# A decode layer whose queries come from a register-addressed loop on TensorE, with two score chunks of the last head rebalanced towards TensorE

**Chip, cores, metric.** One NeuronCore of one Trainium2 chip. Times are device microseconds (us) of one execution; "span" is the time from the first to the last instruction of an execution, 1.7 to 3.0 us shorter. All timed runs told here were in the fast state, at a mean granted TensorE clock of 0.87 to 0.89; e8 and e10 are single runs, whose state can't be told, at 0.88.

## The reference

One decode step: layer norm, attention of one query row over a cache of 32 heads, 32,768 positions and 192 channels, output projection, and a two-layer MLP. All data is bf16.

```python
B, Sq, D = 1, 1, 640;  H, Sk, Dh = 32, 32768, 192;  Dff = 1536
q = (layernorm(x) @ wq).reshape(H, Dh)                  # 640 x 6144 weights
scores = einsum("hd,hkd->hk", q, k_cache) * Dh**-0.5
o = einsum("hk,hkd->hd", softmax(scores), v_cache)
h = x + o.reshape(1, H * Dh) @ wo
out = h + relu(layernorm(h) @ w1) @ w2
```

Keys and values are read once, about 805 of the 825 MB that the kernel loads.

## The kernel before

Everything arrives through one queue of loads, issued in program order by SyncE; a load that overwrites a tile waits for that tile's last reader, and all loads behind it wait too (head 0's second keys are issued at 32.97 us, after the query matmuls, and the load behind them at 33.34). Each head's scores are computed in chunks, and in each chunk some columns are multiplied and reduced on the vector engine while the others are transposed and multiplied on TensorE (with copies by ScalarE).

The query weights borrow tiles that keys and values need shortly after:

```python
wq_c = [kt[1][:, c * H * Dh:(c + 1) * H * Dh] for c in range(DT - 1)] + [va[:, 0:H * Dh]]   # DT = 5 rows
```

so head 0's second half of the keys, which goes to `kt[1]`, waits for `att0`, a signal that comes after the last query matmul:

```python
def keys(h, ld):
    if h > 0:
        ...
        g.wait("scs", h - 1, 4 * ld + 3)
    elif ld == 1:
        g.wait("att0")
    load(kt[ld][:], rows(k_hd, h, P * JK * ld, JK), f"dk{ld}", "k", h, ld)

# order of issue
for c in range(DT):
    load(wq_c[c], ...)                    # five rows of query weights
for h in range(LAST):
    keys(h, 0); vals(h, 0); keys(h, 1)    # head 0's keys(0, 1) is the one that waits
    ...
```

The queries are 5 x 64 matmuls of one column each, unrolled; each loads 96 columns of weights:

```python
for c in range(DT):
    g.wait("wq", c)
    calls = [mmul(o_ps[0:HE, 2*h+e:2*h+e+1], wq_c[c][:, h*Dh+e:(h+1)*Dh:2], xn[:, c:c+1], ...)
             for h in range(H) for e in range(2)]
```

The last head has chunks of its own (tile, offset, columns, columns on TensorE); the even ones up to chunk 3 have 16 on TensorE and 16 on the vector engine:

```python
ends = [(c // 2, (c % 2) * J, J, JPS[c % 2] if c > 3 else 16) for c in range(NC - 2)]   # J = 32, JPS = (20, 16)
ends += [(NL - 1, 0, 20, 12), (NL - 1, 20, 20, 12), (NL, 0, 16, 8), (NL + 1, 0, 8, 8)]
```

TensorE's program there ends with the value matmuls of chunks 5, 6 and 7, then the last softmax denominator (`den`), then chunks 8 and 9.

Of the kernel before, what the change touches and what calls it, by code (L numbers as in the profile page):

```python
# [80 lines left out]
def kernel(  # L81
# [16 lines left out]
    _, H, Sk, Dh = A_k_cache.shape  # L98
# [6 lines left out]
    DT = D // P  # L105
# [3 lines left out]
    J = 32  # L109
    JPS = (20, 16)  # L110
    HE = Dh // 2
    NK = Sk // (P * JK)
    NL = Sk // (P * JL)
    NC = 2 * NL
# [6 lines left out]
    full = [(c // 4, (c % 4) * J, J, JPS[c % 2]) + ((c // 2, (c % 2) * J) if c < 4 else (2, (c - 4) * J)) for c in range(NC)]  # L121

    ENDJ = (40, 16, 8)
    ends = [(c // 2, (c % 2) * J, J, JPS[c % 2] if c > 3 else 16) for c in range(NC - 2)]
    ends += [(NL - 1, 0, 20, 12), (NL - 1, 20, 20, 12), (NL, 0, 16, 8), (NL + 1, 0, 8, 8)]
    ends = [q + q[0:2] for q in ends]
    assert sum(ENDJ) == JL
# [23 lines left out]
    def sbuf(name, shape, dtype, align=32):  # L151
        return ctx.enter_context(nc.sbuf_tensor(name, shape, dtype, align_bytes=align))

    def psum(name, shape, dtype=f32):
        return ctx.enter_context(nc.psum_tensor(name, shape, dtype))


    kt = [sbuf(f"kt{i}", [P, JK * Dh], bf16, 512) for i in range(NK)]
    va = sbuf("va", [P, JK * Dh], bf16, 512)
# [12 lines left out]
    wide = sbuf("wide", [P, HE + P + 2 * (P - HE)], bf16)  # L172
# [16 lines left out]
    ln_t = {}  # L189
    for tag in ("ln1", "ln2"):  # L190
# [3 lines left out]
                         xn=sbuf(f"xn_{tag}", [P, DT], bf16))  # L194
    tp = [psum(f"tp{i}", [P, 4, P]) for i in range(TP)]
    sp = psum("sp", [P, 512])
    o_ps = psum("o_ps", [P, 512])
# [4 lines left out]
    wq_c = [kt[1][:, c * H * Dh:(c + 1) * H * Dh] for c in range(DT - 1)] + [va[:, 0:H * Dh]]  # L202
# [21 lines left out]
    sems = {n: nc.alloc_semaphore(n) for n in names}  # L224
# [90 lines left out]
    def pool_program(g):  # L315
        e = nc.gpsimd
        g.do(lambda: e.memset(wide[:], 0.0), "pool_act", ("ident0",))
        g.wait("ident0")
        g.do(lambda: e.affine_select(out=wide[:], in_=wide[:], compare_op=A.not_equal, fill=1.0, base=HE,
                                     pattern=[[-1, HE + P + 2 * (P - HE)]], channel_multiplier=1), "pool_row", ("ident",))  # L320
        def key(h, ld):
            relay(g, "k", h, ld)
            g.do(lambda: nc.gpsimd.sem_inc(sems["pool_dve"], 1))  # L323
            book_relay(g, "k", h, ld, sem="pool_dve")

        for h in range(LAST):
            key(h, 0)
            relay(g, "v", h, 0)
            key(h, 1)
            for ld in ((2, 1) if h == 0 else (1, 2)):  # L330
                relay(g, "v", h, ld)
            relay(g, "W", h)
        key(LAST, 0)
        relay(g, "v", LAST, 0)
        key(LAST, 1)
        key(LAST, 2)
        relay(g, "v", LAST, 1)

    def relay(g, *label):
        if label[0] != "W":  # L340
            g.wait(*label)
        elif label[1] % 2 == 0:
            g.wait("wo", label[1] // 2)
        g.do(lambda: nc.gpsimd.sem_inc(sems["pool_pe"], 1))  # L344
        book_relay(g, *label)

    def book_relay(g, *label, sem="pool_pe"):
        if g.planning:
            n = g.book["count"].get(sem, 0) + 1
            g.book["count"][sem] = n  # L350
            g.book["at"][("at" if sem == "pool_pe" else "atd",) + label] = (sem, n)
# [4 lines left out]
    def pe_group(g, calls, label, sem="pe"):  # L356
        for fn in calls[:-1]:
            g.do(fn)
        g.do(calls[-1], sem, label)

    def mmul(o, w, r, **kw):
        return lambda: pe.matmul(o, lhsT=w, rhs=r, **kw)  # L362
# [105 lines left out]

    def queries(g):

        for c in range(DT):
            g.wait("wq", c)
            calls = [mmul(o_ps[0:HE, 2 * h + e:2 * h + e + 1], wq_c[c][:, h * Dh + e:(h + 1) * Dh:2],
                          ln_t["ln1"]["xn"][:, c:c + 1], start=(c == 0 and h == 0 and e == 0),
                          stop=(c == DT - 1 and h == H - 1 and e == 1), skip_group_check=True)
                     for h in range(H) for e in range(2)]
            if c < DT - 1:
                for fn in calls:
                    g.do(fn)
            else:  # L480
                pe_group(g, calls, ("q",), "pe_act")

    def q_spread(g, h, turn=None):

# [42 lines left out]
    def pe_start(g):  # L527
        g.wait("identf")
        g.wait("x")
        cols = [x_row[0:1, c:D:DT] for c in range(DT)] + [x_row[0:1, c * P:(c + 1) * P] for c in range(DT)]  # L530
        pe_group(g, [mmul(mm[:, i:i + 1], col, ident_b[0:1, 0:1], start=True, stop=True) for i, col in enumerate(cols)],
                 ("xT",), "pe_dve")
        pe_norm(g)
        g.wait("xn", "ln1")
        queries(g)
        pe_group(g, [mmul(attT[:, 0:DT], ident_b, zero5[:], start=True, stop=False, skip_group_check=True)],
                 ("att0",))
        g.wait("qe")
        q_spread(g, 0)
# [255 lines left out]
    for f in (dma_program, pool_program):  # L795
        f(plan)
# [14 lines left out]
    at = book["at"]  # L811
    ends_at, step = {}, {}
    for e in parts:
        far = {s: 0 for s in TAKEN[e]}
        ends_at[e] = []
        for h in range(LAST):
            for label in logs[e][h]:
                s, n = at[label]
# [11 lines left out]
    def looped(e, eng):  # L830
        start, head, end = parts[e]
        g = Program(book, sems, eng)

        def take(amounts):
            g.flush()
            for s, n in amounts.items():
                eng.sem_inc(sems[s], -n)
                g.sub[s] = g.seen[s] = g.sub.get(s, 0) + n

        start(g)  # L840
        head(g, 0)
        take(ends_at[e][0])
        with eng.Fori(0, LAST - 1) as i:
            if e == "pe":
                head(g, 1, i + 2)
            else:
                head(g, 1)
            take(step[e])
        for s in TAKEN[e]:
            g.sub[s] = g.seen[s] = ends_at[e][LAST - 1][s]  # L850
        g.links = dict(links[e])
        end(g)
        g.flush()

    with nc.Block(name="decode_blk", no_gpsimd_drain=True) as block:
        @block.sync
        def _(eng):
            dma_program(Program(book, sems, nc.sync))

        @block.gpsimd  # L860
        def _(eng):
            pool_program(Program(book, sems, nc.gpsimd))

        @block.scalar
        def _(eng):
            looped("act", nc.scalar)

        @block.vector
        def _(eng):
            looped("dve", nc.vector)  # L870

        @block.tensor
        def _(eng):
            looped("pe", nc.tensor)
# [34 lines left out]
```

## Time and profile before

| | before |
|---|---|
| time, median of the 3 runs at hand for the prediction | 1918.84 us (1917.25 to 1919.17) |
| span of the profiled execution | 1915.5 us |
| loaded | 824.97 MB, one queue, 431 GB/s over the span |
| query matmuls | 7.17 to 32.9 us |
| second half of head 0's keys issued | 32.97 us |

How to read it: the queue of loads is full from the first slice to the last (its packets fill 99.8% of the sixteen engines' span), so the time is the bytes, plus any moment in which nothing is queued, plus the tail after the last landing. Two places matter to the change: the moment at which SyncE may issue the second keys, compared with the moment at which the earlier loads run out, and the tail. The lines that show both stand in the prediction.

### The profile page before, as it was taken

To read this page: it belongs to the slowest core of one execution; us is meant where nothing else is said; L and a number is where in the kernel's file an instruction comes from. 1 tells how busy PE (TensorE), PEld (TensorE's weight loads), DVE (VectorE), ACT (ScalarE), POOL (GpSimd) and SP (SyncE) were. 2 spreads that over 40 slices of the span, in tenths; PEclk is the share of its full clock that TensorE was granted. 3 is DMA by queue.
4 is the path that set the end of the run, shared out by engine and by line. 5 is a ranking of instruction groups with operands and counts; after the bars stand their busy time and mean duration, and the time that the engine had idled before them with its cause. 6 is when DMAs were issued, how large, how long until landed. Compare 5 with 4: busy or idle time off the path is not lost.

```text
span 1915.5 us, 36089 instructions
## 1 busy us (share of the span) xinstructions
PE 1554.6 (81%) x15890; PEld 1091.6 (57%) x15890; DVE 1563.2 (82%) x732; ACT 938.5 (49%) x1998; POOL 1.0 (0%) x6
## 2 busy tenths in 40 slices
PE   7878888887888778887878787878788787777888
PEld 7555555555665555655556555545565555555565
DVE  2797787987878978789787888878798787987897
ACT  2455454554544544545545445445355454554444
POOL 0000000000000000000000000000000000000000
PEclk9888888888978889888899888899888898888988
DMA  9999999999999999999999999999999999999998
GB/s 409 430 434 432 430 438 429 437 435 433 432 434 431 435 432 429 437 430 438 434 430 434 434 432 437 431 429 437 429 437 436 430 436 431 434 433 432 431 432 366
DMA packets 29633, 825.27 MB, mean 431 GB/s; under 512 B 3115, under 2 KB 4652, under 8 KB 8108
## 3 DMA queue, kind: packets, MB, share of 16 engines
q1 hardware_dynamic: 29610, 824.98, 99.8%
q8 instruction: 14, 0.23, 0.0%
q14 instruction: 7, 0.06, 0.0%
q10 hardware_dynamic: 2, 0.00, 0.0%
HBM read 824.97 MB, written 0.00 MB: 431 GB/s over the span
## 4 chain that ended last, share of the span: by engine, by line
DVE 42%; DMA 37%; PE 14%; ACT 5%; issue 1%; DVEq 0%; POOLq 0%; SPq 0%
DMA kt<-in_A_k_cache_dram 35%; DVE sc L701 20%; DVE pr L698 20%; PE tp L381 7%; PE o_ps L362 6%; ACT kT L605 4%; DMA va<-in_A_v_cache_dram 2%; DVE o_pair L713 1%; PE sp L362 1%; ACT pA L620 0%; DVE oT L723 0%; DMA kt<-in_A_wq_dram 0%; DVE rec L706 0%; DVE rec L707 0%; DVE odd L719 0%
## 5 line engine op out<-in xcount | busy, mean ns | idle before, releaser
L698 DVE TENSOR_TENSOR pr<-kt,qb 128x3072 f32<-128x3072 bf16 (+2 forms) x257 | 757.5, 2947 | 314.9 <-POOLq L323 286.8
L605 ACT COPY kT<-tp 128x1024 bf16<-128x1024 bf16 (+1 forms) x897 | 813.8, 1018 | 272.1 <-PE tp L381 272.1
L381 PE MATMUL tp<-ident_f,kt 128*128 128x128 f32 x3453 | 592.3, 333 | 237.8 <-POOLq L344 162.9
L701 DVE TENSOR_REDUCE sc<-pr 128x16 f32<-128x3072 f32 (+2 forms) x257 | 756.8, 2945 | 8.9
L381 PEld LDWEIGHTS tp<-ident_f,kt 128*128 128x128 f32 x3453 | 489.0, 172 | 287.0 <-POOLq L344 168.9
L362 PE MATMUL o_ps<-va,pB 128*2 128x384 bf16 x1150 | 218.4, 337 | 62.4 <-POOLq L344 62.4
L362 PEld LDWEIGHTS sp<-qm,kT 128*128 128x128 bf16 x6906 | 197.6, 98 | 83.4 <-issue 43.7
L362 PE MATMUL sp<-qm,kT 128*128 128x2 bf16 x6906 | 214.6, 164 | 25.6 <-ACT pB L611 24.3
L362 PE MATMUL o_ps<-vb,pB 128*2 128x384 bf16 x1152 | 214.4, 332 | 22.5 <-ACT pA L620 21.9
L620 ACT ACTIVATE pA<-sc 128x16 bf16<-128x16 f32 (+2 forms) x257 | 58.2, 227 | 350.0 <-DVEq L65 350.0
L611 ACT ACTIVATE pB<-sp 128x16 bf16<-128x16 f32 (+2 forms) x258 | 52.4, 203 | 309.7 <-PE sp L362 309.7
L362 PEld LDWEIGHTS o_ps<-va,pB 128*2 128x2 bf16 x1150 | 93.3, 85 | 156.4 <-POOLq L344 70.0
L362 PE MATMUL o_ps<-va,pA 128*2 128x384 bf16 x898 | 173.5, 335 | 0.0
L362 PE MATMUL o_ps<-vb,pA 128*2 128x384 bf16 x896 | 167.9, 328 | 0.0
L362 PEld LDWEIGHTS o_ps<-vb,pB 128*2 128x2 bf16 x1152 | 90.1, 84 | 122.3 <-ACT pA L620 27.5
L362 PEld LDWEIGHTS o_ps<-va,pA 128*2 128x2 bf16 x898 | 77.6, 86 | 76.6 <-issue 10.2
L362 PEld LDWEIGHTS o_ps<-vb,pA 128*2 128x2 bf16 x896 | 75.6, 84 | 71.2 <-issue 1.5
L611 ACT ACTIVATION_READ_ACCUMULATOR pB<-sp 128x1 f32 x258 | 55.1, 214 | 0.0
L620 ACT ACTIVATION_READ_ACCUMULATOR pA<-sc 128x1 f32 x257 | 53.1, 206 | 0.0
L362 PE MATMUL o_ps<-xn_ln,kt 128*96 128x1 bf16 (+1 forms) x316 | 22.4, 208 | 2.6 <-DMA kt<-in_A_wq_dram 2.6
L362 PEld LDWEIGHTS o_ps<-xn_ln,kt 128*96 128x96 bf16 (+1 forms) x316 | 22.2, 176 | 2.8 <-issue 2.7
L713 DVE TENSOR_SCALAR o_pair<-o_ps,rec 2x384 bf16<-2x384 f32 x32 | 19.4, 605 | 2.7 <-PE o_ps L362 1.7
(69 smaller groups left out, 186.7 us busy)
## 6 DMA issues: line engine op xcount, KB each, us to landing
kt<-in_A_k_cache_dram SPq DMA_DIRECT2D x62, 6144.0 KB, 26.7
vb<-in_A_v_cache_dram SPq DMA_DIRECT2D x63, 3072.0 KB, 19.3
va<-in_A_v_cache_dram SPq DMA_DIRECT2D x31, 6144.0 KB, 26.8
kt<-in_A_k_cache_dram SPq DMA_DIRECT2D x3, 3072.0 KB, 22.8
wo_s<-in_A_wo_dram SPq DMA_DIRECT2D x16, 480.0 KB, 19.0
kt<-in_A_wq_dram SPq DMA_DIRECT2D x4, 1536.0 KB, 10.8
va<-in_A_v_cache_dram SPq DMA_DIRECT2D x1, 3072.0 KB, 32.1
va<-in_A_v_cache_dram SPq DMA_DIRECT2D x2, 1536.0 KB, 37.0
```

Of the source, the lines that this page charges most:

```text
L362: return lambda: pe.matmul(o, lhsT=w, rhs=r, **kw)
L381: calls.append(lambda b=b, o=o: pe.transpose(out=dst[:, b, :], in_=src[:, o:o + 2 * P].bitcast(f32), identity=ident_f[:]))
L605: g.do(lambda: act.copy(out=kT[c % 2][:, b0:b0 + nb, :], in_=src[:, 0:nb, :].bitcast(bf16)), "act_pe", ("cp", h, c, k))
L611: g.do(lambda: act.activation(out=pB[c % NB][:, 0:jp], in_=sp[:, 0:jp], func=F.Exp, scale=SCALE, accum_out=dsums[:, 2 * c + 1:2 * c + 2]), ...
L620: g.do(lambda: act.activation(out=pA[c % NB][:, 0:jd], in_=sc[c % NC][:, 0:jd], func=F.Exp, scale=SCALE, accum_out=dsums[:, 2 * c:2 * c + ...
L698: g.chain(lambda: dve.tensor_tensor(out=pr[:, 0:j1 - j0, :], in0=src[:, (off + j0) * Dh:(off + j1) * Dh].rearrange("p (j d) -> p j d", d=D ...
L701: g.chain(lambda: dve.reduce_sum(out=sc[c % NC][:, j0:j1], in_=pr[:, 0:j1 - j0, :], axis=X), "dve")
L713: g.do(lambda: dve.tensor_scalar_mul(out=o_pair[:, :, 1, :], in0=o_ps[0:2, 0:2 * Dh].rearrange("q (i d) -> q i d", i=2), scalar1=rec[0:2, ...
```

## The change

The intent is a shorter program at the start, 256 unrolled matmuls becoming a loop of four turns whose addresses come from a register, and a vector engine that finishes the last head earlier, because chunks 0 and 2 give it 12 columns where it had 16. The core of the diff ("..." marks what is cut: arguments, the branch for the planning pass, the counts of signals for the code after the loop; through the relays GpSimd raises a semaphore by one for each landed row, and each turn waits for that and takes it back):

```diff
-    ends = [(c // 2, (c % 2) * J, J, JPS[c % 2] if c > 3 else 16) for c in range(NC - 2)]
+    ends = [(c // 2, (c % 2) * J, J, JPS[c % 2]) for c in range(NC - 2)]
...
+        for c in range(DT):
+            relay(g, "wq", c)
...
-        for c in range(DT):
-            g.wait("wq", c)
-            calls = [mmul(o_ps[0:HE, 2 * h + e:2 * h + e + 1], wq_c[c][:, h * Dh + e:(h + 1) * Dh:2], ...)
-                     for h in range(H) for e in range(2)]
+        def calls(wq, col):
+            return [mmul(o_ps[0:HE, 2 * h + e:2 * h + e + 1], wq(h * Dh + e), ln_t["ln1"]["xn"][:, col], start=False,
+                         stop=True, skip_group_check=True) for h in range(H) for e in range(2)]
+        n = H * Dh
+        z = wide[0:1, 0:HE]
+        g.do(mmul(o_ps[0:HE, 0:2 * H], z, z[:, 0:2 * H], start=True, stop=True, skip_group_check=True))
...
+            with g.eng.Fori(0, DT - 1) as i:
+                g.eng.wait_ge(sems["pool_pe"], 1)
+                for fn in calls(lambda o: kt[1][:, bass.ds(i * n + o, HE, 2)], bass.ds(i, 1)):
+                    fn()
+                g.eng.sem_inc(sems["pool_pe"], -1)
+        g.wait("at", "wq", DT - 1)
+        pe_group(g, calls(lambda o: va[:, o:o + Dh:2], slice(DT - 1, DT)), ("q",), "pe_act")
```

> **What bounds the kernel now.** I read the page first: engine shares, the slices, the queues.
>
> ```profile
> PE 1554.6 (81%) x15890; PEld 1091.6 (57%) x15890; DVE 1563.2 (82%) x732; ACT 938.5 (49%) x1998; POOL 1.0 (0%) x6
> DMA  9999999999999999999999999999999999999998
> q1 hardware_dynamic: 29610, 824.98, 99.8%
> ```
>
> No engine is full; the one queue of loads is, in every slice. 824.97 MB at 431 GB/s is the whole span of 1915.5 us, so the time is the bytes plus whatever moments the sixteen DMA engines have nothing queued. A change counts only if it makes or removes such a moment, or moves the tail after the last load. The chain of waits (DVE 42%, DMA 37%) names two resources that keep step. So I looked at the start and the end in the timeline.
>
> ```profile
> 3.39 0.48 SPq L232 DMA_DIRECT2D kt<-in_A_k_cache_dram  x1
> 3.91 0.46 SPq L232 DMA_DIRECT2D vb<-in_A_v_cache_dram  x1
> ...
> 7.17 20.61 PE L362 MATMUL o_ps<-xn_ln,kt 128*96 128x1 bf16 x256 [2.61 <-DMA kt<-in_A_wq_dram]
> 27.58 5.23 PEld L362 LDWEIGHTS o_ps<-xn_ln,va 128*96 128x96 bf16 x64
> 27.64 5.26 PE L362 MATMUL o_ps<-xn_ln,va 128*96 128x1 bf16 x64
> ...
> 32.94 0.21 ACT L640 CAST qe<-o_ps 96x64 bf16<-96x64 f32 x1 [27.54 <-PE o_ps L362]
> 32.97 0.33 SPq L232 DMA_DIRECT2D kt<-in_A_k_cache_dram  x1
> 33.34 0.43 SPq L232 DMA_DIRECT2D va<-in_A_v_cache_dram  x1
> ```
>
> Columns: start, length, engine. At 3.91 us the queue has been given five query-weight rows, the first half of head 0's keys and its first values: 5 x 1536 + 6144 + 3072 KB. The next load (second half of the keys) overwrites the tile of the first four weight rows, so it waits until TensorE has finished all 320 query matmuls: 32.97. The landing records of the trace say when that first batch is gone: the values' sixteen parts land between 43.0 and 45.0 us, mean 43.5. So the queue has about 10 us in hand. That slack is what the change spends.
>
> [...] 20.47 us for 256 (7.17 to 27.64) is 80.0 ns each, while 128-column bf16 pairs (sp) follow each other at 25 ns. [...] the register instructions before head h+1's query spread run while older matmuls still drain, so their cost is hidden there. [...]
>
> **The change, part one: the query loop.** Built, it has four turns of 64 x (fused register operation, weight load, matmul), then a semaphore decrement, counter add, compare-and-branch and register move; the fifth row stays unrolled. The 256 matmuls are all still executed; what is new is one sequencer instruction ahead of each. The page does not count these, but the trace records the 60 that the head loop already has, two per head in the query spread: 55 ns (four operations) and 51 ns (three). Between the starts of the two lie one register operation, one weight load by register and one matmul: 132 or 133 ns in 26 heads, 121 in two, 149 in two. The loop's operations are mostly three-operation ones, so one step is estimated at 133 - 4 = 129 ns. This is more than the 80 ns of the array: the stage turns from bound by weight loading to bound by the sequencer[...]. Loop overhead from the head loop's back edge, start to start: decrement 150, add 97, branch 215 + 60, move 97: 0.62 us.
>
> ```profile
> L843 PEldq MOVE  x31: 37/37/39, 93.8 to 1794.0; - x31
> ...
> L843 PEldq ALU_OP  x30: 36/36/42, 153.6 to 1851.7; - x30
> L843 PEldq COMPARE_BRANCH  x30: 83/215/243, 153.7 to 1851.8; - x30
> ```
>
> (min/median/max in ns.) One turn is 64 x 0.129 + 0.62 = 8.88 us, four are 35.5. The rows' weights land at 7.0, 10.7, 14.3 and 19.5 us, so only the first is waited for. [...] Loop: 7.3 to 42.8 us; fifth row at 80 ns: 5.2, to 48.0; the zero matmul that opens PSUM lies before the first row lands and is free; issue of the second keys at about 48.2 instead of 32.97.
>
> A load's first packets come 1.03 us after its issue (first issue 0.96, first packet 1.99), so data flows again at about 49.2. The DMA engines ran out at 43.0 to 45.0: 4.2 us for the last, 5.7 for the mean one. I take **+5.0 us**. Since the queue is at 99.8%, nothing later gives it back. The other work of head 0 starts 12 us later than before (query spread about 49, not 37.7) but the vector engine waits 286.8 us in 32 places for keys, 31.8 of that at the start and about 8 per head, so it catches up within head 0 and 1. The next load that matters, head 1's first keys, comes about 5 us after the third values land, and moves with them.
>
> **Part two: the last head.** Chunks 0 and 2 give 4 of their 16 vector-engine columns each to TensorE. From 16 to 12 columns the multiply falls from 3.36 to 2.56 us and the reduction from 3.35 to 2.55: 1.6 us a chunk, 3.2 in all. TensorE gets 3 more transposes and 6 more score matmuls a chunk, ScalarE one more copy of about 0.9 us; the value matmuls stay 16.
>
> ```profile
> 1864.87 3.36 DVE L698 TENSOR_TENSOR pr<-kt,qb 128x3072 f32<-128x3072 bf16 x1
> ...
> 1884.63 3.36 DVE L698 TENSOR_TENSOR pr<-kt,qb 128x3072 f32<-128x3072 bf16 x1
> ...
> 1886.57 1.46 PE L362 MATMUL o_ps<-va,pB 128*2 128x384 bf16 x8 [0.38 <-POOLq L344]
> ...
> 1902.96 0.29 PE L362 MATMUL mm<-dsums,ones_mat 128*128 128x20 f32 x1 [1.64 <-ACT pA L620]
> ```
>
> Chunk 2 cannot begin earlier: its keys land at 1864.6 and it starts at 1864.87, so chunk 0's saving is lost there but for 0.2. Chunk 2's 1.6 goes through (keys of chunk 4 land at 1871.9, it starts at 1879.33). The vector engine ends 1.8 us earlier. TensorE before the last denominator was idle 1.64 us and gets about 0.45 us later (extra transposes, scores and the copy in front of chunk 3), so the denominator moves by 1.64 - 0.45 = 1.2. Then the last load of w2 (landing 1910.86; its ten matmuls run at about 1911.8) cuts it: about **-1.0 us**.
>
> Sum: 1918.84 + 5.0 - 1.0 = 1922.8 us.
>
> **Rivals.** (a) A matmul with both addresses by register costs the sequencer more. The pairs in the query spread have only one address each, and whether the 133 ns contain 18 ns or 78 ns for the pair depends on how much of the fused operation's own overhead the records leave out. Its neighbours (a counter add of 36 ns, next start 97 ns on; a move of 38 ns, 97 on) leave about 60 ns unrecorded, which speaks for a cheap pair. If each register address cost 60 ns, a step would be about 190 ns, the queries end at 63.6, the gap is about 20 us and the time 1938. I give this one in six. (b) The step is nearer the 121 ns of the first heads, 117 after the correction: queries end at 44.9, the gap is 1 to 3 us, and with the tail the time is about 1920. (c) The loop hides: the slack of 10 us covers it. That needs a step under about 105 ns, which no pair in the trace shows; then only the tail counts, 1917.8. (d) The tail doesn't move, because ScalarE is 96% busy from 1870 to 1880 and the added copies push TensorE past its 1.64 us: +1 us on all of these. [...]
>
> **Range and chances.** The middle is 1922.8; (b) and (c) with run-to-run spread (1917.25 to 1919.17) set the low end at 1918.5; a step of about 155 ns between my estimate and (a) gives 1930, the high end. [...] To be 2% slower (1957) a step would need about 265 ns; to be 2% faster (1880) the kernel would have to move its bytes at a rate that no slice shows. Chances: faster 0.01, within 2% 0.97, slower 0.02.
>
> **What would show each step.** In the changed profile: the 256 matmuls from kt take about 35.5 us, not 20.6, with starts 129 ns apart, a register operation ahead of each; the load of the second keys issued near 48; DMA packets missing for about 5 us between 43 and 49, and the first slice's rate about 409 x (1 - 5/48) = 366 GB/s; the rest of the slices as before. At the end the chunk-0 and chunk-2 rows with 128x2304, chunk 2 still starting with its keys' landing, the last denominator 1.2 us earlier relative to the last w2 landing. The prediction is wrong if the spacing is near 190 ns, if there is no gap in the packets, or if the lost 5 us come back in later heads through DMA slices above 438 GB/s.

The recorded sum is 1918.84 + 5.0 - 1.0 = 1922.8 us; neither of the two terms is cut. Cut, and marked, are passages on the hardware that no trace of this case shows, with a rival (e) that rested on one of them, and the 0.1 us put on the wait's way through GpSimd, an estimate for which no trace was named. Those 0.1 us are still in the loop's start of 7.3 us, and so in the +5.0 (the query matmuls start at 7.17 us before and at 7.38 after). The rest stands on the trace before: the 80.0 ns on 7.17 to 27.64 us, with the weight loads busy for 5.23 of the fifth row's 5.26 us; the hidden register instructions on, for example, those at 137.8 and 137.9 us, while score matmuls run from 137.64 to 138.39; nothing added for a back edge on the head loop's longest branch, 243 ns. That the register operations would not be hidden in the query loop was the author's estimate, from 129 against 80 ns. So are the 0.45 us by which TensorE gets later: three transposes at about 0.11 us (12 in 1.51 us at 138.57) and six score matmuls at 0.025 come to 0.5.

## The result, and the profile after

| | before | after |
|---|---|---|
| time, median of 6 runs each | 1918.28 us (1917.25 to 1919.17) | 1924.76 us (1924.12 to 1926.34) |
| span | 1915.5 us | 1922.3 us |
| fifth row's matmuls start | 27.64 us | 42.83 us |
| second keys issued | 32.97 us | 48.17 us |
| mean landing of the last load (last piece of w2) | 1909.75 us | 1916.35 us |

The ratio is 1.0035, with a 95% interval of 1.0022 to 1.0047: within 2%, but clearly above 1. Ratios are the mean time of one kernel's fast runs over the mean of the other's of the same rounds, so they are not quite the ratio of the medians quoted.

The page of the changed kernel: engine shares (x is the count of instructions), the DMA share in 40 slices, the queue.

```profile
PE 1567.9 (82%) x15909; PEld 1102.1 (57%) x15909; DVE 1560.0 (81%) x732; ACT 940.0 (49%) x2000; POOL 1.0 (0%) x6
DMA  8999999999999999999999999999999999999998
q1 hardware_dynamic: 29610, 824.98, 99.5%
```

The bytes are the same; one digit, the first, has changed from 9 to 8, and the queue's share is 0.3 points lower. 0.3% of 1922 us is about 6 us, and a slice is 48 us long, so this points at the first 48 us. The timeline of the changed kernel at the start (start, length, engine) shows it:

```profile
7.38 8.43 PE L365 MATMUL o_ps<-xn_ln,kt 128*96 x64 [1.12 <-POOLq L347]
16.45 8.48 PE L365 MATMUL o_ps<-xn_ln,kt 128*96 x64 [0.63 <-issue]
25.45 8.33 PE L365 MATMUL o_ps<-xn_ln,kt 128*96 x64 [0.53 <-issue]
34.31 8.34 PE L365 MATMUL o_ps<-xn_ln,kt 128*96 x64 [0.53 <-issue]
42.83 5.27 PE L365 MATMUL o_ps<-xn_ln,va 128*96 128x1 bf16 x64 [0.18 <-issue]
48.17 0.33 SPq L232 DMA_DIRECT2D kt<-in_A_k_cache_dram  x1
```

Four turns, about 9.0 us apart, stand where 5.1 us per row were; the unrolled fifth row still takes 5.27 us. Only the first turn waits for a landing; the others start after "issue" (0.53 to 0.63 us), that is, after nothing that the profile shows as a wait. The view of the matmul helper's line from 5 to 45 us names the new instruction (durations in ns, minimum/median/maximum):

```profile
L365 PEldq FUSED_REGOPS  x256: 46/46/79, 7.2 to 42.3; - x128
L365 PE MATMUL o_ps<-xn_ln,kt x256: 232/235/236, 7.4 to 42.4; 128*96 x128
```

One register operation stands ahead of each of the 256 matmuls. The starts of successive looped matmuls are 124 ns apart in most places; with some longer ones (154) the mean is (8.43 - 0.235) / 63 = 130 ns in the first turn and 129.6 over the four.

What the late issue does to the transfers is in the windows view (stretch, its length, then busy time and count of PE, PEld, DVE, ACT, POOL, then the TensorE clock, the DMA share and GB/s). Before:

```profile
43.00:49.00 6.00, 4.41 (x41) 2.80 (x38) 5.93 (x2) 5.97 (x11) 0.00 (x0) 1.00 0.99 430
```

After:

```profile
40.00:43.00 3.00, 2.82 (x23) 2.73 (x24) 0.00 (x0) 0.00 (x0) 0.00 (x0) 1.00 0.88 377
43.00:49.00 6.00, 5.73 (x74) 5.64 (x74) 0.00 (x0) 0.21 (x1) 0.00 (x0) 1.00 0.01 4
49.00:55.00 6.00, 6.00 (x52) 5.99 (x51) 5.32 (x3) 5.36 (x8) 0.00 (x0) 1.00 1.06 401
```

For six microseconds nothing moves: share 0.01, 4 GB/s. Integrated over the packet records, the sixteen engines are idle for 6.3 us between 42 and 50 us. Nor do they return at full rate: with each packet's bytes spread evenly over its own duration, 310, 322 and 404 GB/s in the microseconds from 50 on, against about 433 otherwise, worth some 0.7 us more. About 0.4 us comes back around 80 us, where the kernel before has a small dip of its own. From head 1 to the last weights every load lands 6.6 us later than before, without drift over 30 heads: what is lost at 43 us is, but for those 0.4 us, neither recovered nor multiplied. (The scale of chance: a second profile of the kernel before, e8 below, has its landings within 0.05 us of the first's up to 176 us, and 0.5 to 0.8 us later from there on.)

The tail's timeline after, with the vector engine's last score reduction and TensorE's last denominator:

```profile
1870.85 2.56 DVE L711 TENSOR_TENSOR pr<-kt,qb 128x2304 f32<-128x2304 bf16 x1 [1.59 <-POOLq L326]
...
1905.15 1.75 DVE L714 TENSOR_REDUCE sc<-pr 128x8 f32<-128x1536 f32 x1
1909.35 0.81 PE L365 MATMUL o_ps<-vb,pA 128*2 128x384 bf16 x4
1910.09 0.40 PE L365 MATMUL mm<-dsums,ones_mat 128*128 128x20 f32 x2
```

The same reduction in the timeline of the kernel before:

```profile
1900.77 1.75 DVE L701 TENSOR_REDUCE sc<-pr 128x8 f32<-128x1536 f32 x1
```

Such starts must be read against the landing of the last load, because everything has moved. The scores end 7.23 us ahead of that landing before (1902.52 against 1909.75) and 9.45 us ahead after: 2.2 us gained. But the denominator starts 6.79 us ahead before and 6.26 ahead after: 0.5 us lost. Before, TensorE waited 1.64 us for the vector engine's last chunk; after, it comes straight from the value matmuls, with no bracketed wait. In this profile TensorE has become the one that is late. The time went to the queue's gap at 43 us, 6.6 us of it; the tail gave nothing.

### The profile page after: what moved, and what is told of

Read it like the earlier page. It is cut to its first block, busy times and chain, and to the rows that moved or that the text cites. A ratio compares the mean times of both kernels' runs of the same rounds, so it can differ in the third digit from the quotient of the medians.

```text
span 1922.3 us, 36406 instructions
## 1 busy us (share of the span) xinstructions
PE 1567.9 (82%) x15909; PEld 1102.1 (57%) x15909; DVE 1560.0 (81%) x732; ACT 940.0 (49%) x2000; POOL 1.0 (0%) x6
## 4 chain that ended last, share of the span: by engine, by line
DMA 39%; DVE 39%; PE 16%; ACT 4%; issue 1%; DVEq 0%; POOLq 0%; SPq 0%
DMA kt<-in_A_k_cache_dram 34%; DVE sc L714 18%; DVE pr L711 18%; PE o_ps L365 8%; PE tp L384 7%; DMA va<-in_A_v_cache_dram 5%; ACT kT L618 4%; PE sp L365 1%; DVE o_pair L726 1%; ACT pA L633 0%; DVE oT L736 0%; DMA kt<-in_A_wq_dram 0%; DVE rec L719 0%; DVE rec L720 0%; DVE odd L732 0%
## 5 line engine op out<-in xcount | busy, mean ns | idle before, releaser
L711 DVE TENSOR_TENSOR pr<-kt,qb 128x2304 f32<-128x2304 bf16 (+2 forms) x257 | 755.9, 2941 | 322.5 <-POOLq L326 250.9
L714 DVE TENSOR_REDUCE sc<-pr 128x12 f32<-128x2304 f32 (+2 forms) x257 | 755.2, 2939 | 8.9
L365 PE MATMUL o_ps<-vb,pB 128*2 128x384 bf16 x1154 | 217.2, 335 | 23.8 <-ACT pA L633 23.2
L633 ACT ACTIVATE pA<-sc 128x12 bf16<-128x12 f32 (+2 forms) x257 | 58.2, 227 | 358.7 <-DVEq L65 358.7
L624 ACT ACTIVATE pB<-sp 128x20 bf16<-128x20 f32 (+2 forms) x258 | 52.4, 203 | 299.7 <-PE sp L365 299.7
L365 PE MATMUL o_ps<-xn_ln,kt 128*96 (+1 forms) x316 | 35.2, 221 | 2.9 <-issue 1.7
L365 PEld LDWEIGHTS o_ps<-xn_ln,kt 128*96 (+1 forms) x316 | 34.4, 143 | 3.7 <-issue 3.2
```

The source lines that it names most:

```text
L365: return lambda: pe.matmul(o, lhsT=w, rhs=r, **kw)
L624: g.do(lambda: act.activation(out=pB[c % NB][:, 0:jp], in_=sp[:, 0:jp], func=F.Exp, scale=SCALE, accum_out=dsums[:, 2 * c + 1:2 * c + 2]), ...
L633: g.do(lambda: act.activation(out=pA[c % NB][:, 0:jd], in_=sc[c % NC][:, 0:jd], func=F.Exp, scale=SCALE, accum_out=dsums[:, 2 * c:2 * c + ...
L711: g.chain(lambda: dve.tensor_tensor(out=pr[:, 0:j1 - j0, :], in0=src[:, (off + j0) * Dh:(off + j1) * Dh].rearrange("p (j d) -> p j d", d=D ...
L714: g.chain(lambda: dve.reduce_sum(out=sc[c % NC][:, j0:j1], in_=pr[:, 0:j1 - j0, :], axis=X), "dve")
```

## The experiments

Theory: of the 6.5 us, all comes from the loop, through the gap in the queue; within the loop the cost is the register operation ahead of every matmul, not the loop nor an address held in a register; and the chunks bring nothing because TensorE takes over as the bound of the last head. Each timed run has 5 runs of its own and 9 of the kernel before on the same chip. Medians of the kernel before: 1918.33 us for e1 to e4, 1918.03 for e5 to e7, 1918.54 for e9.

### The change in two halves: e1 and e2

e1 is the changed kernel with the old chunks; e2 is the kernel before with the new chunks.

```diff
# e1, against the changed kernel
-    ends = [(c // 2, (c % 2) * J, J, JPS[c % 2]) for c in range(NC - 2)]
+    ends = [(c // 2, (c % 2) * J, J, JPS[c % 2] if c > 3 else 16) for c in range(NC - 2)]
# e2, against the kernel before: the same line the other way round
```

> The kernel before with the query loop alone; the last head's chunks stay as before. Theory: the whole loss comes from the loads that run dry between 43 and 49 us, 6.3 us of idle queue and about 0.4 us of slow restart in the trace of the changed kernel, so the time is before plus 6.6, with the tail left as it was: 1924.9 us (1924.2 to 1925.6), second keys issued at 48.2, mean landing of every load from head 1 on 6.6 us later than in the kernel before. Rival: part of the loss is the last head's chunks (their TensorE path got 2 us later in the trace); then this run is about 1 us better than the changed kernel, near 1923.7.

> The kernel before with the last head's chunks 0 and 2 at 20 TensorE columns, queries unrolled as before. The prediction's term was -1.0 us: 1917.3. Theory after the trace: the vector engine ends 1.4 to 1.8 us earlier, but TensorE's own order and the last landing of the feed-forward weights take over, so the time is that of before within 0.5: 1917.8 to 1918.8. Rival: the added transposes and copies cost the end about 1 us: 1919.3.

e1: 1924.04 us, ratio 1.0028 (1.0015 to 1.0042); second keys issued at 48.02, loads 6.4 us later. e2: 1918.21 us, ratio 0.9998 (0.9984 to 1.0011). The loop alone makes 5.7 us of medians; that is a little under the range that I expected for e1, between the theory and its rival, but 6.4 of the 6.6 us of lateness in the landings are there. The chunks move the time by nothing that five rounds can see. These times can't tell 0 from the prediction's -1.0 us, since e2's interval reaches from -3.1 to +2.1 us; what the chunks do is read from the profiles of the tail below.

### What in the loop costs: e3

The loop stays, and its weight address still comes from a register, but all 64 matmuls of a turn use the same address, so there is one register operation per turn. The queries are wrong on purpose.

```diff
-                for fn in calls(lambda o: kt[1][:, bass.ds(i * n + o, HE, 2)], bass.ds(i, 1)):
+                for fn in calls(lambda o: kt[1][:, bass.ds(i * n, HE, 2)], bass.ds(i, 1)):
```

> The changed kernel with one and the same weight address by register for all 64 matmuls of a turn: one register operation a turn instead of 64, both operands still addressed by register; the queries are wrong on purpose. Theory: it is the register operation ahead of each matmul that costs, the address by register costs nothing: starts 80 ns apart as in the unrolled code, a turn 5.8 us instead of 8.9, second keys issued at 36, no dry queue, 1917.8 to 1918.8 us. Rival: reading addresses from registers slows the sequencer: starts stay near 124 ns, issue at 48, 1924.8 us.

1917.43 us, ratio 0.9992 (0.9979 to 1.0006), with less left of the loop than I expected: a turn takes 5.1 us, not 5.8. The output even stays within the tolerance of the comparison, so a passing comparison proves little about the queries here. Its timeline at the start:

```profile
7.40 20.63 PE L365 MATMUL o_ps<-xn_ln,kt 128*96 x256 [1.14 <-POOLq L347]
...
33.22 0.33 SPq L232 DMA_DIRECT2D kt<-in_A_k_cache_dram  x1
```

256 matmuls in 20.63 us, 80 ns each, in one unbroken group (the view no longer parts them into turns): the rate of the unrolled kernel, whose line in the prediction has 20.61. Two register-held addresses per matmul, the branch, the semaphore wait and the decrement of each turn add 0.02 us to it in all. The loop costs 0.25 us in the issue of the second keys, and the register operations are what costs 15 us of TensorE's time. Rival (a) of the prediction, a price per register address, falls here too. (e3 also makes all loads of a turn read the same weights; the unrolled kernel, which reads different ones, has the same 80 ns, so that is not what the speed comes from.)

### How much loop the slack covers: e5 and e6

The first two or three rows in the loop, the rest unrolled from `kt[1]` as before.

```diff
-            with g.eng.Fori(0, DT - 1) as i:
+            with g.eng.Fori(0, 2) as i:          # e5; 3 in e6
 ...
+        for c in range(2, DT - 1):               # e5; from 3 in e6
+            g.wait("at", "wq", c)
+            for fn in calls(lambda o: kt[1][:, c * n + o:c * n + o + 2 * HE - 1:2], slice(c, c + 1)):
+                g.do(fn)
```

> The changed kernel with only the first two weight rows in the loop; rows three to five unrolled. Theory (the loop costs 3.8 us a row, and only what exceeds the queue's slack is lost): loop 7.4 to 25.4 us, three unrolled rows of 5.1 to 40.8, second keys issued at 41.0, first packets at 42.0, before the queue is dry at about 42.9: no gap, time as the kernel before within 0.7: 1917.6 to 1919.0 us. Rival (each looped row costs its share of the 6.5 us): 1921.5 us.

> Three rows in the loop, two unrolled. Theory: queries end at 44.6, issue at 44.8, first packets at 45.9: 2.9 us without data and some 0.6 us of slow restart, so 3 to 3.6 us over the kernel before: 1921.5 us; mean landings from head 1 on shifted by the same 3.0 to 3.6 us. Rival (a share per row): 1923.2 us.

e5: 1917.75 us, ratio 0.9999 (0.9986 to 1.0013). e6: 1921.10 us, ratio 1.0014 (1.0000 to 1.0028), loads 3.5 us later. The timeline of e5:

```profile
16.36 8.48 PE L365 MATMUL o_ps<-xn_ln,kt 128*96 x64 [0.64 <-issue]
25.00 10.39 PE L365 MATMUL o_ps<-xn_ln,kt 128*96 128x1 bf16 x128 [0.17 <-issue]
40.58 0.33 SPq L232 DMA_DIRECT2D kt<-in_A_k_cache_dram  x1
```

Two looped turns and two unrolled rows; the issue at 40.58 is 2.4 us before the queue runs dry at about 43, and the gap does not exist. In e6 the issue comes at 44.48, and in its windows view the stretch after 43 us has lost part of its transfers:

```profile
43.00:46.00 3.00, 2.73 (x31) 2.65 (x31) 0.19 (x1) 0.60 (x3) 0.00 (x0) 1.00 0.66 205
```

So two rows cost nothing (-0.3 us of medians), three 3.1, four 6.5: not a share per row, but slack first and then about one microsecond of time for each microsecond of lateness. From e6 to the changed kernel the issue is 3.7 us later and the median 3.4 to 3.7 us longer.

### Taking the wait away: e4, and e7 with cheap addresses

If the gap is the cost, the same loop should be free where nobody waits for its tile. In e4 the weights lie in the value tiles, so head 0's second keys are queued at once and its first values wait instead.

```diff
-    wq_c = [kt[1][:, c * H * Dh:(c + 1) * H * Dh] for c in range(DT - 1)] + [va[:, 0:H * Dh]]
+    wq_c = [va[:, c * H * Dh:(c + 1) * H * Dh] for c in range(DT - 1)] + [vb[:, 0:H * Dh]]
 ...
-            elif ld == 1:
-                g.wait("att0")
 ...
+            if h == 0:
+                keys(h, 1)
+                g.wait("att0")
+                vals(h, 0)
```

> The changed kernel with the first four weight rows in the tile of the later values and the fifth in the tile of the first values; head 0's second keys are queued at once, and the first values wait for the queries instead. The loop is as slow as in the changed kernel. Theory: only the dry queue costs. The queue now holds 20.4 MB instead of 17.3 MB, dry at about 49 to 50 us, first values issued at 48.2 and flowing at 49.3: gap under 0.5 us, 1918 to 1919 us, although the queries end as late as ever. Rival: the late queries delay head 0's compute and this costs by itself: 1922 to 1925 us.

A miss, in the range of the rival: 1922.64 us, ratio 1.0024 (1.0010 to 1.0037). The windows view of e4 says that the gap did close and where another opened:

```profile
43.00:49.00 6.00, 5.73 (x74) 5.64 (x74) 0.00 (x0) 0.21 (x1) 0.00 (x0) 1.00 0.98 426
80.00:85.00 5.00, 4.74 (x57) 2.96 (x56) 4.97 (x2) 4.46 (x11) 0.00 (x0) 1.00 0.69 245
```

From 43 to 49 us the transfers run at 426 GB/s, where the changed kernel had 4; but from 80 to 85 they fall to 245. The timeline names the load concerned, head 1's first keys, and what it waited for last, TensorE's value matmuls of head 0's chunk 4. In e4 they end at 83.68:

```profile
82.54 1.14 PE L372 MATMUL o_ps<-va,pA 128*2 128x384 bf16 x6
...
83.71 0.33 SPq L232 DMA_DIRECT2D kt<-in_A_k_cache_dram  x1
```

and in the kernel before they had waited only for the landing of their values:

```profile
74.01 3.36 PE L362 MATMUL o_ps<-va,pB 128*2 128x384 bf16 x10 [4.88 <-POOLq L344]
...
78.97 0.33 SPq L232 DMA_DIRECT2D kt<-in_A_k_cache_dram  x1
```

In e4 head 0 is late. The vector engine could not begin before the queries were there (49.6 us) and, working almost without a pause, ends chunk 3 at 73.8; ScalarE waits 1.89 us for it before its next copies of transposed keys; so TensorE begins the value matmuls of chunk 4 only at 80.91. The queue is dry from 81.3. Behind the first gap lay a second bound: late queries make head 0 late. Part of the loss could also be the new placement, which delivers the first values late. So e7 takes e4's placement with e3's single address per turn (queries wrong on purpose again); the edit is those two diffs together.

> The weight rows in the value tiles as in the fourth experiment, but with one register operation a turn, so that the queries end at about 33 instead of 48 us (wrong queries on purpose). Theory: what that experiment lost, 4.7 us, came from head 0's compute starting at 48.5 us: head 1's first keys were issued at 83.7 with the queue dry from 81.3. With the queries early the keys are issued at 77 to 80, no gap: 1917.5 to 1919 us. Rival: the placement itself costs (first values only 58 us in): 1922 to 1923 us.

1920.13 us, ratio 1.0008 (0.9995 to 1.0022), median 2.1 us over that of the kernel before, again over what I expected, though the interval doesn't exclude no loss at all; loads are 1.7 us later, and head 1's first keys are issued at 80.71. So of e4's 4.7 us of lateness in the landings, about 1.7 go with the placement (in e7 TensorE waits 14.09 us for the first values, until 59.64). The other 3.0 are not all due to the late queries: 1.89 are ScalarE's wait, which e7 does not have, and about 1.1 come from the clock, which stayed reduced from 59 to 65 us in e4 (ten value matmuls from 59.65 us take 3.36 us, where ten from 80.91 take 1.79) and was back before 63 in e7. This split is read from one trace of each. In the changed kernel this second bound is invisible, because a gap of the same cause has already given head 0 its time back.

### The tail: e8, e9, e10

One trace of each kernel cannot tell a denominator that is always late from one that was late once. e8 is the kernel before once more, e10 is e2 once more, both unchanged, for one profile each.

> The kernel before, unchanged, for a second profile of its tail. In its first profile TensorE was idle 1.64 us before the last denominator; in three of the other profiles a half-clock window of 3.4 us fell on the third group of last-head values and TensorE, not the vector engine, set the denominator. Theory: [...] the last denominator then lies 5.9 to 6.8 us before the mean landing of the last load here too, with TensorE's idle time before it anywhere from 0 to 1.7 us. Rival: the kernel before always has that idle time, 1.5 to 1.8 us.

> The kernel of the second experiment once more for a second profile of its tail. Theory: the vector engine's scores end 9.0 to 9.5 us before the mean landing of the last load and the last denominator again 5.2 to 6.4 us before it, TensorE idle under 0.2 us ahead of it. Rival: the late denominator was chance: 6.6 us or more before the landing.

e8: 1917.88 us; e10: 1918.34 us. Times relative to the mean landing of the last load, in us:

| kernel | scores end on the vector engine | TensorE's wait ahead of the last denominator | denominator starts | last engine's landing | output issued |
|---|---|---|---|---|---|
| before | -7.23 | 1.64 | -6.79 | +1.10 | +3.43 |
| before again (e8) | -7.13 | 0.56 | -6.69 | +1.20 | +3.27 |
| old chunks, loop (e1) | -7.73 | none | -6.61 | +1.40 | +3.65 |
| after | -9.45 | none | -6.26 | +2.02 | +3.65 |
| new chunks (e2) | -9.37 | none | -5.91 | +2.03 | +4.01 |
| new chunks again (e10) | -8.89 | none | -7.84 | +1.95 | +3.39 |
| new chunks, lighter TensorE (e9) | -5.73 | 1.89 | -5.29 | +1.13 | +4.66 |

e8 is as its theory had it (a clause of it on the clock, not shown at that point, is cut; what the traces show of the clock follows below): the same kernel has a wait of 0.56 us, not 1.64. The vector engine gains about two microseconds (1.2 to 2.3) in the changed kernel, e2 and e10, and in each of them TensorE has no wait left. But it has none in e1 either, with the old chunks, so a lost wait is not the mark of the new chunks alone. When the denominator then comes is not settled by the kernel: -5.91 in e2, -7.84 in e10, the same program. e10 fell outside what I expected for it (-5.2 to -6.4), where its rival, chance, had put it. Its timeline:

```profile
1902.15 0.81 PE L362 MATMUL o_ps<-vb,pA 128*2 128x384 bf16 x4
1902.90 0.40 PE L362 MATMUL mm<-dsums,ones_mat 128*128 128x20 f32 x2
```

What differs is the clock in this stage, which is reduced for a while in e2 and in the changed kernel. In the windows view of the changed kernel the clock (third number from the end) falls below 1 for two stretches:

```profile
1893.00:1896.00 3.00, 2.61 (x11) 1.03 (x10) 2.85 (x2) 2.10 (x7) 0.00 (x0) 0.65 1.02 434
1896.00:1899.00 3.00, 3.00 (x25) 1.43 (x24) 2.96 (x2) 0.27 (x2) 0.00 (x0) 0.78 0.96 401
```

A reduced-clock stretch of 3.4 us begins at 1893.9, and ten value matmuls take 3.19 us where they otherwise take 1.79. In e2 a stretch of 10.2 us reaches 3.5 us into these value matmuls; in e10 one of 6.8 us ends 3.8 us ahead of them. From the first of them to the denominator TensorE takes 14.7 us in e10 and e5, where no reduced clock falls on them, and 16.4 us in e1, e2 and the changed kernel, where it does (16.1 to 17.0 in e3, e4, e6 and e7). So a stretch here costs about 1.7 us, with either chunks. It is not all of the scatter: e5, at full clock for the last 40 us before the landing, begins these matmuls 1.5 us later than e10, and its denominator lies at -6.33; why stays open.

In each trace the changes of the granted clock, between 1 and 0.5, lie on a grid of 3.413 us (142 in the kernel before, 128 in the changed one), and its offset from the first instruction differs (3.36 us in the kernel before, 2.94 in the changed one, 2.29 in e8). That offset alone does not decide the run, though: it is 0.28 us in e2 and 0.33 in e10.

And where the denominator was early, in e10, the output still came at +3.39: the slowest DMA engine landed 1.95 us after the mean, and the output cannot come before it. The chain that ended last in e10 (critical view) leads back to that load, issued at 1895.66 and complete at 1912.69:

```profile
1895.66 17.03 DMA kt<-in_B_w_dram
```

What a late TensorE costs is seen in e3's profile, the slowest of its five runs (1920.46 us, the others 1917.30 to 1917.93): its last load lands only 0.4 us later than in the kernel before, but the denominator starts at -3.76, and the output is issued at +6.17, where the kernel before has +3.43.

e9 asks whether TensorE is the bound, by giving it less: chunks 6 and 7 of e2 with 8 instead of 12 columns on TensorE.

```diff
-    ends += [(NL - 1, 0, 20, 12), (NL - 1, 20, 20, 12), (NL, 0, 16, 8), (NL + 1, 0, 8, 8)]
+    ends += [(NL - 1, 0, 20, 8), (NL - 1, 20, 20, 8), (NL, 0, 16, 8), (NL + 1, 0, 8, 8)]
```

> The kernel before with chunks 0 and 2 at 20 TensorE columns and, to take work off TensorE and ScalarE at the end, chunks 6 and 7 at 8 columns instead of 12. In the profiles so far the kernels with the new chunks end the vector engine's scores 9.0 to 9.5 us before the mean landing of the last load (old chunks 7.1 to 7.7), but their last denominator comes 5.2 to 6.3 us before it (old 6.6 to 6.8), with TensorE busy up to it. Theory: TensorE with its copies is what the new chunks overload; here the scores end about 7.8 us and the denominator 6.5 to 7.0 us before that landing, time within 0.5 us of the kernel before: 1917.3 to 1918.3 us. Rival: the clock window and the landing alone set the denominator: it stays 5.2 to 6.3 us before the landing.

1919.10 us, ratio 1.0002 (0.9988 to 1.0015). The time is within noise of the kernel before, though over my range. The wait is back at TensorE, in e9's timeline:

```profile
1904.85 0.40 PE L362 MATMUL mm<-dsums,ones_mat 128*128 128x20 f32 x2 [1.89 <-ACT pA L620]
```

TensorE was relieved, as expected, but my size was wrong: I counted the vector engine's extra 1.6 us once, and it is 1.6 us per chunk, 3.2 in all. The scores therefore end at -5.73, not -7.8, and the vector engine is the bound again. The denominator at -5.29 is where the rival had put it, but with 1.89 us of waiting for the vector engine ahead of it, which is not the rival's reason. The two engines are within a microsecond or two of each other here, so moving four columns of two chunks either way swaps the bound.

No version beat the kernel before. e5 equals it with 64 matmuls fewer in the program (the 128 of two rows become a loop body of 64).

## Why the prediction was right or wrong, point by point

**The bound** (right): the queue of loads, and a gap in it as the price. The first digit of the DMA row is the only one that changed, and the first slice's rate, put at 366 GB/s, is 360.

**The step of the loop** (right): 129 ns were predicted from the query spread's pairs; 129.6 ns is the mean of the four turns. That the two agree so closely is partly luck: the mean is made of 124 in most places and some longer ones, which were not foreseen, and the register operation itself is recorded at 46 ns, not 51. The turn was put at 8.88 us and is 8.98; the second keys' issue was put at 48.2 and is 48.17.

**"I take +5.0 us"** (mechanism right, this term mis-sized): it was taken between 4.2 us for the last engine and 5.7 for the mean one, as if the last engine set the pace. What counts is idle capacity summed over all sixteen. The mean of 43.5 that I used hid that about thirteen engines were done by 43.0 to 43.4, and the few that finished at 44.8 carried almost nothing. Measured: 6.3 us idle, 0.7 of slow restart that I had not counted, 0.4 given back near 80 us, together 6.6.

**"Since the queue is at 99.8%, nothing later gives it back"** (right but for those 0.4 us): all later landings keep the same 6.6 us.

**"about -1.0 us" for the chunks** (wrong): e2's median is only 0.1 us under the kernel before, which alone would not decide; but in all eight profiles with the prediction's chunks (the changed kernel, e2 to e7, e10) the output is issued 3.39 to 6.17 us after the mean landing of the last load, in the three with the old ones (before, e8, e1) 3.27 to 3.65. The first links were right: chunk 2 did wait for its keys (1.59 us at 1870.85), and the vector engine did finish about two microseconds earlier (1.8 predicted). The step that failed is "the denominator moves by 1.64 - 0.45 = 1.2": it took TensorE's 1.64 us of waiting, read from one trace, as slack that the change could use. In e8 the same kernel has 0.56, in e1 none, and with the prediction's chunks it is gone in all eight profiles, with the start of the denominator left to TensorE's own load and clock. And the next step failed with it: in e10 the denominator does come 1.1 us earlier, and the last landing takes all of it, not the 0.2 us that the prediction allowed for.

**The rivals.** (a), 60 ns per address: fell; e3 has two register addresses per matmul at 80 ns. (b), 121 ns a step: fell as a time, though the commonest step of 124 is near it. (c), the slack hides it: fell for four rows, and is exactly what two rows do (e5). (d), the tail doesn't move because the added copies fill TensorE: the outcome came true, with TensorE's wait gone; that the copies are the reason is not shown, since the last run of value matmuls begins 22.0 to 23.2 us ahead of the landing with the old chunks and 22.3 to 22.6 in the changed kernel, e2 and e10. The overhead of a turn, put at 0.62 us, is 0.76 to 0.87 us between last and first matmul, one step included, and is not seen in e3, where the 256 matmuls of the four turns take 20.63 us.

The sum, 1918.84 + 5.0 - 1.0, so missed both terms in the same direction, by 1.6 and 1.0 us. The base, a median of three runs, happened to lie 0.6 us over that of six (1918.28), which hid part of this; the middle lies 2 us under the measured 1924.76, inside the range.

## What to carry to other kernels

A loop whose addresses come from a register was free here (0.25 us) while its instructions shared the register's value; a register operation ahead of every small matmul took a stage from 80 ns a step, with the weight loads busy for 5.23 of 5.26 us of a row, to 130 ns. Price a delay at the head of a queue of loads as slack first, then as idle time summed over all DMA engines, and look for the next bound behind the first before moving buffers. A wait seen in one trace is not slack to spend: look at a second trace, and at who is late when the wait is gone.

## Also measured

- A register operation ahead of a matmul with a computed address is recorded at 46 ns, makes a step of 124 ns (130 in the mean), and costs nothing when it is one per 64 matmuls (e3, 80 ns a step).
- A compare-and-branch in the head loop is recorded at a median of 215 ns on TensorE in the kernel before (208 in the changed one), at 45 on ScalarE and 56 on VectorE in both.
- TensorE's head loop, with 974 recorded instructions a turn, has a branch of at most 243 ns at its 30 back edges, and in e3 the turns of the small loop follow each other at 80 ns.
- From the start of SyncE's issue the first packet takes 1.03 us in the kernel before and 0.95 after the gap; from the end of the issue it is 0.62 us in both. After the gap the queue comes back slowly: 310, 322 and 404 GB/s in the microseconds from 50 on, against 433 (in e4, after the gap at 83 us, 302, 320 and 379).
